# One core, three networks in a row: the overflow branch one expert earlier, weight splits in halves, the scaling behind the last hl, and a new order at the first expert

## The chip, the cores and the metric

One core of a Trainium2 chip runs the whole program in one launch. The metric is the device time of an execution in microseconds; the profiled execution also gives a span, from its first to its last instruction. TensorE is called PE in the rows (PEld is its weight load), VectorE DVE, ScalarE ACT, GpSimd POOL, and SP issues most DMAs.

## The reference

Three computations follow each other, all in float32: a recurrent attention (4 batches, 8 heads, 768 positions, 40 channels a head), a network of eight experts of which each token uses one, and a network shared by all 3072 tokens. Cut to what matters here:

```python
def _moe_ref(x, w_gate, w_output_gate, w1, w2):        # x: 3072 x 320
    logits = x @ w_gate
    e_idx = np.argmax(logits, axis=1)
    ...                                                 # gate_w: softmax of the best, eom: sigmoid
    for e in range(8):
        mask = e_idx == e
        h = np.maximum(x[mask] @ w1[e], 0.0)            # 320 -> 1024
        ye = h @ w2[e]                                  # 1024 -> 320
        out[mask] = gate_w[mask, None] * eom[mask, e, None] * ye

def _moe2_ref(x, w_in, w_out, alpha):
    h = x @ w_in                                        # 320 -> 2048
    g = np.maximum(h, 0.0) + alpha * np.minimum(h, 0.0)
    return g @ w_out                                    # 2048 -> 320
```

## The kernel before, in words

Float32 products are made of fast ones: each operand is split into a rounded part (hi, hh, xh) and the rest (lo, hl, xl), and three products of the parts are summed. ScalarE makes the rounded part by a copy, VectorE the rest by a subtraction. So every weight matrix is loaded raw by a DMA (`raw`, three buffers), then split by a *job* (`piece.split`: one ScalarE copy, L309, and one subtraction, L310). A job that is done issues the next load. Jobs of the next expert run during the present one. `conv` jobs turn the shared network's 64-bit weights into float32 on the way and write them back to memory from GpSimd's queue (L330 to L332).

Tokens are first routed. Each group of tokens goes through the steps `best` (one-hot of the best expert, small VectorE operations), `count` (two matmuls with the one-hot, L156), `place` (row numbers, L166 to L175), `scatter` (an indirect DMA from GpSimd to the rows of the buffer `xs`, L177), then `sums` and `scale` (the factor `sc`). Only the last groups are routed behind the attention, in `go`, between the first expert's steps (`route`).

The experts are *blocks* of 8 steps f, of 448 tokens each; expert 0 has 384 tokens as the first block and 128 as the ninth. The shared network then runs as six blocks c of 512 tokens and 16 steps. In `run` a step is: first-layer matmuls into one of three hp buffers (`mm1`, L394), the activation with its split into hh and hl (L399 and L402 for experts, L408 to L411 for the shared network), the second-layer matmuls (`mm2`, L421) of the step two before, and then the hooks of this f: jobs, loads, transposes of the next block's x (`xparts`: L383, L384, L386), and so on. Engines work strictly in the order in which this is written down, and SP's and GpSimd's DMAs start in that order too.

Behind expert 7 all steps are drained, and `overflow` stands there: a count is read into a register of every engine, and if it is over zero, tokens beyond an expert's room are worked off; with these inputs the branch is not entered. Then `gather2` fetches the first 512 tokens of the shared network from `xs` by four indirect DMAs (L508), which must wait for expert 7's last store (L472), while the short ninth block runs. `sc0` scales them by `sc` (L514, and a copy of 64 columns, L515), the ninth block is drained at once (`flush`), and their transposes follow. In later blocks the same is done with the next 512 tokens: gather at f=0, scaling at f=4, transposes at f=6, 9 and 12 into a buffer of their own (`tp`).

## Time and profile before

| | us |
|---|---|
| three runs | 975.82, 979.36, 985.04 |
| median | 979.36 |
| the profiled execution, its own time | 975.97 |
| its span | 974.20 |
| TensorE busy in the span | 923.4 (95%) |
| VectorE, ScalarE, GpSimd busy | 758.5, 401.5, 157.0 |
| mean granted clock of TensorE | 0.978 of 2.4 GHz |

Until about 376 us the attention runs, which the change leaves alone; the first expert's block until 405, the others until 595, the short ninth block until 613, then the shared network. Busy matmul time is modelled at its end, so a stretch that looks full of matmuls can still hold time that they wait; the distance from one step's first matmul to the next tells more.

### The profile page before, as it was taken

Reading aid. Unit: us, or ns where it says so; the run is one execution under the profiler, and the core shown is the slowest. Engines: PE = TensorE matmul, PEld = TensorE weight load, DVE = VectorE, ACT = ScalarE, POOL = GpSimd, SP = SyncE. Lnnn points to the kernel's source line nnn. Section 1 sums busy time; section 2 is a strip of 40 time slices with the busy share of each in tenths; the row PEclk is TensorE's granted clock in tenths of the full one; section 3 lists DMA queues with packets and bytes.
Section 4 is the critical chain, followed back from the end, with each engine's and each line's share of the span. In section 5 each row is a group of like instructions: output and inputs, shape, how many; then the busy total and the mean of one; then the engine's idle time right before and its main releaser. Section 6 shows DMA issues by size and latency. Waiting matters only on the chain. (4 is left out here: it accounts for less than half of the span.)

```text
span 974.2 us, 26737 instructions
## 1 busy us (share of the span) xinstructions
PE 923.4 (95%) x11176; PEld 840.7 (86%) x11176; DVE 758.5 (78%) x1715; ACT 401.5 (41%) x823; POOL 157.0 (16%) x246
## 2 busy tenths in 40 slices
PE   6479999999999999999999999999999999999998
PEld 5368888888888889899999998879999999999997
DVE  7999999999998556788888885776766666666664
ACT  3745545555553454565556554332121221222211
POOL 1000000111022114144434453101010010100000
PEclk7689999999999999999999999999999999999999
DMA  4435886444434652767677776310010010000000
GB/s 126 122 105 160 247 254 189 128 123 141 136 78 102 197 149 96 256 208 249 221 236 242 236 231 207 101 45 28 28 28 28 1 54 1 28 28 1 28 1 27
DMA packets 59582, 118.45 MB, mean 122 GB/s; under 512 B 7684, under 2 KB 34500, under 8 KB 59460
## 3 DMA queue, kind: packets, MB, share of 16 engines
q1 hardware_dynamic: 55412, 103.04, 35.0%
q0 software_dynamic: 4048, 13.69, 4.2%
q8 instruction: 88, 1.44, 0.6%
q14 instruction: 34, 0.28, 0.1%
HBM read 90.24 MB, written 26.46 MB: 120 GB/s over the span
## 5 line engine op out<-in xcount | busy, mean ns | idle before, releaser
L394 PE MATMUL hp<-xh,w 128*128 128x512 f32 (+3 forms) x1008 | 298.1, 378 | 0.1
L421 PE MATMUL yp<-w,hh 128*128 128x320 f32 (+1 forms) x1280 | 284.4, 309 | 0.7 <-ACT hh L410 0.7
L421 PEld LDWEIGHTS yp<-w,hh 128*128 128x128 f32 (+1 forms) x1280 | 216.9, 185 | 11.6 <-ACT hh L410 2.3
L394 PEld LDWEIGHTS hp<-xh,w 128*128 128x128 f32 x1008 | 187.6, 189 | 26.6 <-issue 0.4
L421 PE MATMUL yp<-w,hl 128*128 128x320 f32 x584 | 181.4, 311 | 3.9 <-DVE hl L402 2.7
L410 ACT CAST hh<-g 128x512 fp32r<-128x512 f32 x96 | 59.5, 620 | 275.4 <-PE yp L421 148.4
L394 PE MATMUL hp<-xl,w 128*128 128x512 f32 (+3 forms) x336 | 127.0, 378 | 0.2 <-DVE xl L386 0.2
L411 DVE TENSOR_TENSOR hl<-g,hh 128x512 fp32r<-128x512 f32 x96 | 66.5, 693 | 72.8 <-ACT hh L410 72.0
L421 PEld LDWEIGHTS yp<-w,hl 128*128 128x128 f32 x584 | 109.6, 188 | 6.3 <-DVE hl L402 3.4
L408 DVE TENSOR_SCALAR g<-hp,al 128x512 f32<-128x512 f32 x96 | 71.8, 748 | 39.8 <-PE hp L394 39.8
L310 DVE TENSOR_TENSOR w<-raw,w 128x1024 fp32r<-128x1024 f32 (+3 forms) x65 | 87.5, 1347 | 17.8 <-ACT w L309 15.5
L409 DVE SCALAR_TENSOR_TENSOR g<-hp,g 128x512 f32<-128x512 f32 x96 | 66.4, 691 | 3.3
L394 PEld LDWEIGHTS hp<-xl,w 128*128 128x128 f32 x336 | 63.4, 189 | 5.7 <-DVE xl L386 0.6
L309 ACT CAST w<-raw 128x1024 fp32r<-128x1024 f32 (+1 forms) x66 | 64.3, 976 | 8.2 <-DMA raw<-W 8.1
L692 DVE TENSOR_TENSOR tmp<-S 128x30 f32<-128x30 f32 (+27 forms) x258 | 63.6, 271 | 1.0
L694 DVE TENSOR_TENSOR S<-S,tmp 128x30 f32<-128x30 f32 (+27 forms) x258 | 63.6, 271 | 0.9
L508 POOL DMA_INDIRECT xg<-xs,pos x24 | 25.9, 1078 | 226.5 <-PE tp L383 167.8
L819 PE MATMUL Pp<-rz,xt 128*128 128x128 f32 x384 | 55.3, 287 | 0.0
L789 ACT COPY x<-W 32x320 f32<-32x320 f32 x96 | 40.0, 417 | 30.4 <-PE W L786 26.9
L399 ACT ACTIVATE hh<-hp 128x448 fp32r<-128x448 f32 (+2 forms) x72 | 36.7, 509 | 36.4 <-issue 22.8
L819 PEld LDWEIGHTS Pp<-rz,xt 128*128 128x128 f32 x384 | 46.4, 191 | 2.5 <-issue 0.2
L820 DVE TENSOR_TENSOR x<-Pp,mask 128x512 f32<-128x512 f32 x48 | 32.4, 686 | 18.0 <-PE Pp L819 15.9
(169 smaller groups left out, 1362.9 us busy)
## 6 DMA issues: line engine op xcount, KB each, us to landing
raw<-W SPq DMA_DIRECT2D x45, 512.0 KB
x<-VX SPq DMA_DIRECT2D x48, 232.0 KB
xs<-z SPq DMA_DIRECT2D x17, 480.0 KB
fm<-FM SPq DMA_DIRECT2D x46, 160.0 KB
raw<-WI SPq DMA_DIRECT2D x10, 512.0 KB
raw<-WO SPq DMA_DIRECT2D x10, 512.0 KB
vv<-VM SPq DMA_DIRECT2D x24, 160.0 KB
rz<-R SPq DMA_DIRECT2D x48, 80.0 KB
```

Source lines behind the costliest of these rows:

```text
L309: s.nc.scalar.copy(hi,r[0][:,0:n])
L310: (eng or s.nc.vector).tensor_tensor(lo,r[0][:,0:n],hi.bitcast(F32),SUB)
L394: for i,(l,r) in enumerate(seq): nc.tensor.matmul(hp,l,r,start=(i==0),stop=(i==len(seq)-1))
L408: nc.vector.tensor_scalar(g,hp,0.0,s.al[:,f:f+1],ALU.min,MUL)
L409: nc.vector.scalar_tensor_tensor(g,hp,0.0,g,ALU.max,ADD)
L410: nc.scalar.copy(hh,g)
L411: nc.vector.tensor_tensor(hl,g,hh.bitcast(F32),SUB)
L421: nc.tensor.matmul(yp[j][o],l,r[:,f],start=(f==0 and i==0),stop=(f==nf-1 and i==len(p)-1))
L692: V.tensor_tensor(t3[0][:,r],S[:,r,j:j+1].to_broadcast([P,n,w]),S[:,j:j+1,j+1:].to_broadcast([P,n,w]),MUL)
L694: for r in parts(split): V.tensor_tensor(S[:,r,j+1:],S[:,r,j+1:],t3[0][:,r],ADD)
L789: k=nc.scalar.copy(x[bl,sd,:,64:192].rearrange("p a (j d) -> p a j d",j=2)[:,:,:,0:40],W[bl].rearrange("p (a j) d -> p a j d",j=2))
L819: nc.tensor.matmul(Pp[:,2*qq:2*qq+2],xt[:,qq,128*sd:128*sd+128],rz1[:,:,qq,sd],start=True,stop=True)
```

## The change

It has six parts, all in the part behind the attention.

1. `overflow` is called behind expert 6 instead of expert 7, so that the blocks are run as 0 to 6, branch, 7, and then the rest.
2. In the last step of a block with a tail of 64 tokens `mm2` does the tail first, and `done` copies and stores it first.
3. Expert 7's eight jobs go to f = 0, 0, 1, 2, 2, 3, 4, 5 instead of one to each f. The three jobs of the ninth block are split in halves of 512 columns, one at each f from 0 to 5, and two of its three loads go to the beginning of the shared network.
4. The scaling of the first 512 tokens stands behind the activation of the ninth block's last step (`soon`), half on VectorE and half on ScalarE. In the shared network all scaling is on ScalarE, at f = 9 to 12 of its first block, behind the weight splits, and at f = 5 to 8 of the later ones.
5. The transposes of the next 512 tokens stand together at f=13, two of the three parts in hp buffers.
6. At the first expert the transposes of its x stand ahead of `best`, and `count` and `place` move into the block's second step. The first piece of its second weight is split in two parts on VectorE, not on GpSimd and ahead of the block. The load of expert 1's rows goes from GpSimd's queue to SP's; the transposes of these rows stand together at f=6.

```diff
-            i=(nc.gpsimd if e==1 else nc.sync).dma_start(out=xg[0:m,js,0:D],in_=src)
+            i=nc.sync.dma_start(out=xg[0:m,js,0:D],in_=src)
...
-        def split():
-            hi,lo=dst()
-            s.nc.scalar.copy(hi,r[0][:,0:n])
-            (eng or s.nc.vector).tensor_tensor(lo,r[0][:,0:n],hi.bitcast(F32),SUB)
+        def split(a=0,b=n):
+            hi,lo=dst(); c=slice(a,b)
+            s.nc.scalar.copy(hi[:,c],r[0][:,c])
+            s.nc.vector.tensor_tensor(lo[:,c],r[0][:,c],hi[:,c].bitcast(F32),SUB)
...
+    def part(s,a,b,end=True):
+        s.jobs[s.ndone][1](a,b); s.ndone+=end
...
-        for j in range(J):
+        for j in range(J) if f<nf-1 or n%128==0 else (J-1,*range(J-1)):
...
                 late.append((b,f,b["act"](hp,f)))
+                for fn in b.get("soon",{}).get(f,[]): fn()
                 while len(late)>(0 if f==b["nf"]-1 and b.get("flush") else 2): fin()
...
         s.push(s.mix(s.wexpert(1),s.convs(0)))
-        s.job()
...
+        for fn in X[0][2]: fn("hp")
         while rq[0][1].__name__!="count": route()
-        for fn in X[0][2]: fn("hp")
-        route()
         s.pre()
...
-                for dst,m,js in r:
+                for dst,m,js in r[::-1]:
...
             if e==0:
-                hooks[0].append(lambda: route())
-                hooks[1].append(lambda: route(1000))
-                hooks[1].append(lambda: load(1)); hooks[4].append(lambda: next(cnt))
+                hooks[0].append(lambda: s.part(0,D,False))
+                hooks[1]+=[lambda: route(4),lambda: s.part(D,1024),s.load]
+                hooks[2].append(lambda: load(1)); hooks[3].append(lambda: route(1000)); hooks[4].append(lambda: next(cnt))
...
-            n=6+len(s.convs(e)) if e<NE else 3
-            for i in range(n+2 if e==0 else n): hooks[(1,2,3,4,5,6,7,7)[i] if e==0 else (i*8+7)//n if e<NE else i].append(s.job if e<NE else lambda: s.job(False))
+            n=6+len(s.convs(e)) if e<NE else 0
+            if e==NE:
+                for i in range(6): hooks[i].append(lambda i=i: s.part(512*(i%2),512*(i%2)+512,i%2))
+                hooks[1].append(s.load)
+            for i in range(n+2 if e==0 else n): hooks[(2,2,3,4,5,6,7,7)[i] if e==0 else (0,0,1,2,2,3,4,5)[i] if e==NE-1 else (i*8+7)//n].append(s.job)
             if e==0:
-                for k in (2,1,0): hooks[(6,7,7)[k]].insert(0,lambda k=k: X[1][2][k](('tp','tp','hp')[k]))
+                for k in (2,1,0): hooks[6].insert(0,lambda k=k: X[1][2][k](('tp','hp','hp')[k]))
...
-        s.run(blocks[:NE])
+        s.run(blocks[:NE-1])
         s.overflow()
+        s.run(blocks[NE-1:NE])
...
-                nc.vector.tensor_scalar(xg[:,j,0:D],xg[:,j,0:D],s.sc[:,n:n+1],None,MUL)
-                nc.vector.tensor_copy(xg[:,j,D:384],xg[:,j,256:D])
+                if c or j%2:
+                    nc.scalar.activation(xg[:,j,0:D],xg[:,j,0:D],AF.Copy,scale=s.sc[:,n:n+1])
+                    nc.scalar.copy(xg[:,j,D:384],xg[:,j,256:D])
+                else:
+                    nc.vector.tensor_scalar(xg[:,j,0:D],xg[:,j,0:D],s.sc[:,n:n+1],None,MUL)
+                    nc.vector.tensor_copy(xg[:,j,D:384],xg[:,j,256:D])
...
-        for f in (3,4,5): blocks[NE]["hooks"][f].append(s.load)
-        for j in range(4): blocks[NE]["hooks"][min(j+5,7)].append(lambda j=j: sc0(j))
+        blocks[NE]["soon"]={7:[lambda j=j: sc0(j) for j in range(4)]}
...
-                if c==0: s.job()
+                if c==0: s.load(); s.load(); s.job()
...
-                hooks[4]+=[lambda sc=sc,j=j: sc[0](j) for j in range(4)]
-                for k in range(3): hooks[6+3*k].append(lambda k=k,c=c: X[NE+2+c][2][k]())
+                for j in range(4): hooks[j+(5 if c else 9)].append(lambda sc=sc,j=j: sc[0](j))
+                hooks[13]+=[lambda k=k,c=c: X[NE+2+c][2][k](tags[k]) for k in range(3)]
```

On SP's queue behind the attention (`raw` are weights, `xg` the rows of expert 1), before:

```order
L212 DMA xa<-xs 128x3x320
L306 DMA raw<-W 128x1024 x5
L306 DMA raw<-W 128x512
L306 DMA raw<-W 128x1024 x2
L317 DMA raw_7482<-WI 128x1024
```

and now:

```order
L212 DMA xa<-xs 128x3x320
L306 DMA raw<-W 128x1024
L212 DMA xg<-xs 128x3x320
L212 DMA xg<-xs 64x320
L306 DMA raw<-W 128x1024 x4
```

The load of expert 1's rows, which GpSimd issued, now stands behind one weight load and ahead of all others.

On VectorE at the end of the ninth block (`hl` of its last steps, `xg` the gathered rows), before:

```order
L402 SCALAR_TENSOR_TENSOR hl<-hp,hh 128x128 x3
L514 TENSOR_SCALAR xg<-xg,sc 128x320
L515 COPY xg<-xg 128x64
L402 SCALAR_TENSOR_TENSOR hl<-hp,hh 128x128
L514 TENSOR_SCALAR xg<-xg,sc 128x320
L515 COPY xg<-xg 128x64
L402 SCALAR_TENSOR_TENSOR hl<-hp,hh 128x128
L514 TENSOR_SCALAR xg<-xg,sc 128x320
```

and now:

```order
L310 TENSOR_TENSOR w_9803<-raw,w_9802 128x512
L404 SCALAR_TENSOR_TENSOR hl<-hp,hh 128x128 x2
L523 TENSOR_SCALAR xg<-xg,sc 128x320
L524 COPY xg<-xg 128x64
L523 TENSOR_SCALAR xg<-xg,sc 128x320
L524 COPY xg<-xg 128x64
L388 TENSOR_TENSOR xl<-tp,xh 128x512 x2
```

No hl stands behind a scaling any more, and only two of the four scalings are left there.

On SP from expert 7's stores to the shared network's weights (`wi`, `wo`), before:

```order
L306 DMA raw<-wi_65 64x1024 x2
L472 DMA xs<-yo 128x320 x3
L472 DMA xs<-yo 64x320
L235 TENSOR_LOAD nbi
L306 DMA raw<-wo_66 128x3x320 x2
L306 DMA raw<-wi_65 128x1024
L473 DMA xs<-yo 128x320
```

and now:

```order
L306 DMA raw<-wi_65 64x1024 x2
L473 DMA xs<-yo 64x320
L473 DMA xs<-yo 128x320 x3
L306 DMA raw<-wo_66 128x3x320
L474 DMA xs<-yo 128x320
L306 DMA raw<-wo_66 128x3x320
L306 DMA raw<-wi_65 128x1024 x2
```

The read of the count (L235) is gone from here, and two of three weight loads went behind the ninth block's own store (L473 before, L474 now).

## Rows read from the trace of the kernel before

**Rows 1.** Stages: window, length, PE, PEld, DVE, ACT, POOL busy (count), clock, DMA share, GB/s.

```profile
376.00:405.00 29.00, 26.43 (x162) 24.44 (x161) 20.52 (x50) 15.55 (x31) 10.04 (x18) 1.00 0.49 161
405.00:595.00 190.00, 190.00 (x1141) 181.53 (x1139) 157.12 (x274) 108.16 (x180) 81.18 (x78) 1.00 0.72 232
595.00:613.00 18.00, 14.54 (x102) 13.37 (x102) 8.84 (x22) 7.08 (x17) 4.87 (x4) 0.93 0.60 197
613.00:655.00 42.00, 40.03 (x201) 32.65 (x201) 32.77 (x49) 14.31 (x20) 3.83 (x4) 0.99 0.27 80
```

**Rows 2.** Timeline, first expert: start, duration, engine, line, operation [idle before <-releaser].

```profile
377.86 0.39 PE L156 MATMUL pr<-ohs,one 128*128 128x16 f32 x2 [0.83 <-DVE ohs L153]
379.94 2.40 POOL L310 TENSOR_TENSOR w<-raw,w 128x1024 fp32r<-128x1024 f32 x1 [1.52 <-ACT w L309]
381.04 1.33 DVE L166 TENSOR_TENSOR add<-tot,base 128x8 f32<-128x8 f32 x1
...
385.43 0.96 POOL L177 DMA_INDIRECT xs<-xu,pos  x1 [0.21 <-issue]
...
388.50 1.38 POOL L212 DMA_DIRECT2D xg<-xs  x2 [2.03 <-PE hp L394]
...
396.29 0.83 PE L383 MATMUL tp<-ident,xg 128*128 128x128 f32 x4 [1.10 <-DMA xg<-xs]
```

**Rows 3.** Two-microsecond windows at the end of the ninth block, columns as in rows 1.

```profile
608.00:610.00 2.00, 0.06 (x1) 0.06 (x1) 0.90 (x4) 0.00 (x0) 0.00 (x0) 1.00 0.37 142
610.00:612.00 2.00, 1.92 (x10) 1.68 (x11) 0.98 (x5) 1.01 (x2) 0.00 (x0) 0.65 0.15 54
612.00:614.00 2.00, 2.00 (x8) 1.73 (x7) 1.67 (x3) 1.61 (x3) 0.79 (x1) 0.50 0.08 28
```

**Rows 4.** Timeline, from expert 7's end to the shared network's first transposes.

```profile
594.68 0.46 PE L421 MATMUL yp<-w,hh 128*64 128x320 f32 x2
594.88 0.43 ACT L470 COPY yo<-yp 128x320 f32<-128x320 f32 x1 [0.45 <-PE yp L421]
...
600.69 1.98 POOL L508 DMA_INDIRECT xg<-xs,pos  x1 [7.62 <-DMA xs<-yo]
...
605.52 0.96 POOL L508 DMA_INDIRECT xg<-xs,pos  x1 [0.30 <-issue]
...
609.07 0.39 DVE L514 TENSOR_SCALAR xg<-xg,sc 128x320 f32<-128x320 f32 x1 [1.93 <-DMA xg<-xs,pos]
...
609.60 0.28 DVE L402 SCALAR_TENSOR_TENSOR hl<-hp,hh 128x128 fp32r<-128x128 f32 x1
...
609.94 0.41 PE L421 MATMUL yp<-w,hl 128*128 128x320 f32 x1 [2.02 <-DVE hl L402]
610.19 2.75 PE L383 MATMUL tp<-ident,xg 128*128 128x128 f32 x12
```

**Rows 5.** The chain that ended last, at expert 7's last store: start, length, what.

```profile
596.29 3.46 DMA xs<-yo
```

**Rows 6.** The line L508: the gathers' time from issue to landing.

```profile
DMA to landing us min/median/max: 2.9/3.1/4.4
```

**Rows 7.** Timeline, shared network: VectorE's and TensorE's steps, later transposes.

```profile
612.59 0.77 PE L394 MATMUL hp<-xh,w 128*128 128x512 f32 x1
...
618.52 0.74 DVE L408 TENSOR_SCALAR g<-hp,al 128x512 f32<-128x512 f32 x1
...
620.56 0.39 PE L394 MATMUL hp<-xh,w 128*128 128x512 f32 x1
...
622.71 0.74 DVE L408 TENSOR_SCALAR g<-hp,al 128x512 f32<-128x512 f32 x1
...
624.15 0.39 PE L394 MATMUL hp<-xh,w 128*128 128x512 f32 x1
...
657.34 0.45 PE L421 MATMUL yp<-w,hh 128*128 128x320 f32 x2
662.69 0.60 PE L383 MATMUL tp<-ident,xg 128*128 128x128 f32 x4
```

## What I predict

> **What bounds the kernel now.** I read the stages first [rows 1]. TensorE is busy in every stage behind the attention, and where it isn't, it waits for something that this change touches: 2.57 of 29.00 us idle around the first expert, none in 190 us over the experts after it, 3.46 of 18.00 us at the passage to the last network. The first block of the last network shows 1.97 us idle, but there busy time hides more (below). So all that can be gained behind the attention lies in three places, and 190 us of dense matmuls can only lose.
>
> First place [rows 2]: at 377.86 TensorE has waited 0.83 us for the one-hot, because the routing's small VectorE steps stand ahead of the split of x. At 396.29 it has waited 1.10 us for the second expert's rows. Their load went out on GpSimd's queue at 388.50, when the last scatter (385.43) had landed, and took until 396.3 beside weight loads. GpSimd's split of weights ran from 379.94 for 2.40 us, and VectorE's first step of the placement, which moves 128x8, took 1.33 us beside it.
>
> Second place [rows 4, 5]: the last expert's matmuls end at 594.68+0.46 = 595.14; its last store is issued at 596.29 and lands 3.46 us later; the gathers start at 600.69 and the fourth at 605.52; one landing ends only at 609.07. In VectorE's order the last hl of the short block stands behind that scaling (609.60), so TensorE waits 2.02 us until 609.94 and transposes from 610.19. Then its clock is down: 0.65 and 0.50 in the two stretches of 2 us after the one with 0.06 us busy [rows 3]. That is the 1.2 GHz level for some 4 us. The wait of 1.10 us at 396.29 brought no such drop: the clock of its whole stage is 1.00 [rows 1].
>
> Third place [rows 7]: a step of the last network is 3.59 us on TensorE (620.56 to 624.15), but 4.19 us on VectorE when it also splits weights (618.52 to 622.71; the rest of the nine such steps repeat it, 4.2 to 4.3). The lead of two steps is used up after three. From the second-layer matmuls of f=1 (1.83 us after 620.56, so 622.39) to those of f=9 (657.34) TensorE needs 34.95 us; eight steps of 3.59 and two groups of transposes at 0.44 would be 29.6. So 5.3 us go there, though the matmul view shows them mostly as stretched matmuls.
>
> **The change part by part.**
>
> First expert. The transposes' split now stands ahead of the best-of search, and counting goes behind the second step. TensorE gets 0.83 us earlier to the first matmul, but the split itself (three VectorE steps of 0.5 us) still ends about 0.4 us after; and the two counting matmuls (0.47 us) move, they don't vanish. I take 0.4 us. The weights' split leaves GpSimd; VectorE pays about 1.2 us for it in two parts (0.4 before, 0.8 behind the placement) and gets back the 1.17 us of the slowed step. Nothing of that is on TensorE's path: its second-layer matmuls start some 2 us later. The second expert's load moves to SP's queue: there it waits for the scatters and **holds every weight load behind it**, all of the second expert's but the first. Scatter to landing took 3.1 us (385.43 to 388.50); the scatters come about 0.4 us earlier. The load then goes ahead of two weight loads (0.56 and 1.0 MB), at some 340 GB/s about 391 instead of 396.3, so the 1.10 us go. Late are now the weights: the second piece at about 392.5, the third at about 394. ScalarE is in order, so the seventh hh waits behind the third piece's cast, and the grouped transposes use two of the three hp buffers, so the eighth step's first matmul waits for that hl: my sum has it at 397.2 instead of 395.8. Of the 2.57 us idle and some 0.9 us of stretched matmuls I count **2.0 us** as gained; bounds 0.5 (scatters land 1.2 us later) and 3.2 (weights come in time).
>
> Overflow branch. It moves from behind expert 7 to behind expert 6. That drains TensorE once at each end, where it was pipelined before; the drained steps need hl of the last step 3.2 us after its matmul, and VectorE has two short splits in between, so I price the drain at 0. Work is what it was. Expert 7's eight splits move into its first six steps; counting 1.2 us per split, 2.4 per conversion and 0.8 per hl, VectorE ends each hl 1.2 to 2 us ahead of need. Queued behind the branch on SP are four of expert 7's loads, behind expert 6's store; they need their buffer anyway, about 2 us after SP is through. I take **-0.3 us** for one contended step; bounds 0 and -3.
>
> Passage. The tail of 64 rows is now copied and stored first, so the last store waits for one ScalarE copy (0.43 us, like the one at 594.88 [rows 4]): 595.65 instead of 596.29. Only one weight load is in flight beside it instead of three, and two of the next three stand behind the short block's own store. Landing: between 2.9 (the best gather) [rows 6] and the 3.46 seen; I take 3.0, so 598.65. First gather 0.94 us later, as seen (599.75 to 600.69): 599.6. The fourth follows 4.83 us later as seen, or 3.8 without the first one's double time (1.98 us): 603.4 to 604.4. Landing 3.1, the median [rows 6], gives 606.5 to 607.5. Scaling of the last quarter on ScalarE with its copy: 0.43+0.2 and a handover, 0.8, so 607.3 to 608.3. TensorE without its stalls would be at the transposes at 610.19-3.2 = 607.0; hl no longer waits for a gather. Three transposes fit in, then 0.3 to 1.3 us are left to wait, too short by the row above for the clock to fall. The twelve transposes took 2.40 us at the lower clock (610.19 to 612.59, the next matmul), about 1.05 us at the upper. The last network's first matmul comes at 608.1 to 609.0: **4.0 us** gained, bounds 1 and 4.8.
>
> The ScalarE step itself is not in the trace of before. The Trainium skill ("ScalarE: Activation LUTs", Rules for kernel authors) says to use VectorE, not ScalarE, for a multiply, and in What ACT_TABLE_LOAD costs gives 186 ns plus 0.833 ns an element, with 93 ns for a pointer operand: as an estimate from that page 0.55 us for 320 columns and 0.24 for 64, so 0.79 instead of my 0.63, and the sum would be 0.2 us less. No run here shows it yet.
>
> First block of the last network. Scaling leaves VectorE (four times 0.39+0.20 [rows 4] = 2.4 us), and the split of the next x moves behind the weights, to f=13. VectorE's chain decides until f=9: its first step came 5.5 us after the transposes' start (618.52-2.82-610.19); at the upper clock I take 4.55. Then 2.87 us each for f=0 and 1, 4.19 (four times), 4.31 (three times), 3.5 with the last, short split: hl of f=9 at 43.5 us, its matmuls 0.3 before. Counted from the network's first matmul, 1.05 us in, that is 42.1 us; before it was 657.34-612.59 = 44.75. Then twelve transposes and a wait for the hp buffer, 1.35, against the one group left before, 0.44: **1.7 us** gained. It is not the whole 5.3: 3.5 us of it are the eight weight splits, which stay. ScalarE's four scalings (0.63 each by my price above) stand at f=9 to 12, behind the steps with a weight split, and fit beside the activation's copy, so it is no new bound. Bounds 0.5 and 4.
>
> Later blocks. Transposes in one group instead of three save two switches, about 0.2 us in each of four (0.60 us busy for a group of four [rows 7]); scaling was hidden before and is now: **0.8 us**, bounds -1 and 1.
>
> **Sum.** 2.0-0.3+4.0+1.7+0.8 = 8.2 us. The profiled execution took 975.97 us (span 974.20 and 1.77 around it), so 967.8. That is at the fast end of the three runs shown (975.82 to 985.04); their median is 3.4 above it. I put half of that on top: **969 us**.
>
> **The rivals.**
> A. *The gather still ends last.* All its parts stay as seen: 595.65+3.46+0.94+4.83+4.4 (the worst landing [rows 6]) is 609.3, scaling 610.1: no earlier than now, one idle stretch of 3 us and the lower clock again. What is left is 2.0-0.3+1.7+0.8, 4.2: 971.8 by the profile, 973.5 with the shift. For it: three loads were seen beside the slow landings, one is still there. Chance 0.18.
> B. *The weights come late.* Four loads behind the scatters in expert 0, or behind SP's branch in expert 7, cost what rows 2 gave: 0.5 and -3 there and 4.0 in all: 972.0, or 973.7. Chance 0.12.
> C. *More of the third place goes*, since with the scaling gone the lead of two steps lasts longer: 3.5 us more, 964.3, or 966. Chance 0.1.
> D. *Slower: the hp ring stops the last network.* The grouped transposes take two of the three hp buffers in five blocks. The matmuls of f=14 need the buffer of f=13; TensorE is there 2.8 us after f=13 (1.75+1.05), VectorE frees it 1.44 us (0.75+0.69) after it starts on it. The slack is 1.4 us. It costs whatever VectorE lags beyond that, in each block; the whole gain is used up at 8.2/5 = 1.6 us, so it decides from a lag of 3.0. In the first block I have a lag of 1.6 there; later ones split no weights and VectorE needs 2.9 of 3.59 us. At a lag of 5 it would be 975.97-8.2+18 = 986. Chance 0.06.
> That the change moves nothing (the stores' order and the branch being without effect) is in A.
>
> **How the numbers follow.** The forecast has 0.54. A measurement of this kernel tells about 1%, 9.8 us, from no change; the shown runs differ by as much. My 8.2 by the profile or 10 by the median lies on that border: of the forecast and C about 0.4 are faster by over 1%; A, B and the rest of the forecast are within; D and a bad spread give slower 0.05. The range runs from 2 us under C on the profile's base (962; the bounds of the first two places allow them) to A and B with the whole gap to the median on top (977).
>
> **What would show it.** Right: the second expert's load lands before 392 and TensorE's wait at the first expert's transposes is under 0.5 us; expert 7 stays dense; the gathers start before 600 in terms of before; the transposes run at clock 1.00, with hl ahead of the scaling; the step of the first shared block is still 4.2 us on VectorE but no transposes wait for scaling. Wrong: a wait over 1.5 us at the transposes (A), ScalarE waiting for raw weights in experts 0 or 7 (B), TensorE waiting at f=14 in each block (D).

## The result, and the profile after

The changed kernel takes 982.42 us in the median of 20 runs (978.02 to 991.03), the kernel before 977.23 (973.81 to 985.04). The ratio is 1.0056, with a 95% interval of 1.0039 to 1.0074: **slower by half a per cent**, where 1% faster was forecast.

Both profiles are cut at the same five groups of matmuls, each taken by its start in the timeline: (A) from the first expert's own transposes to the first transposes that stand in the second expert's block; (B) the six periods of 8 steps from there to the first transposes in expert 7; (C) from there to the ninth block's first matmul; (D) the passage, to the last network's first matmul; (E) to the end of the span.

| us | ahead of A | A | B | C | D | E | span |
|---|---|---|---|---|---|---|---|
| before | 375.88 | 38.40 | 164.19 | 16.82 | 17.30 | 361.61 | 974.20 |
| after | 376.44 | 42.96 | 167.99 | 20.98 | 14.91 | 359.62 | 982.90 |
| difference | +0.56 | +4.56 | +3.80 | +4.16 | -2.39 | -1.99 | +8.70 |
| forecast | 0 | -2.0 | 0 | +0.3 | -4.0 | -2.5 | -8.2 |

Over the 20 profiles of this study the stretch ahead of A, which no kernel here changes, ran from 370.95 to 381.59, so a single execution carries up to 10 us that the change has no part in. Each part is therefore read below from its own stage.

**A.** The timeline of the changed kernel in the first expert; here [rows 2] had a wait of 0.83 us and one of 1.10.

```profile
378.10 0.44 PE L396 MATMUL hp<-xh,w 128*128 128x384 f32 x1 [0.51 <-DVE xl L388]
...
383.82 0.16 DVE L175 TENSOR_TENSOR pos<-pl,m 128x2 int32<-128x2 f32 x1
...
384.75 0.96 POOL L177 DMA_INDIRECT xs<-xu,pos  x1 [5.71 <-ACT w L309]
...
386.01 1.21 POOL L177 DMA_INDIRECT xs<-xu,pos  x1 [0.21 <-issue]
...
389.90 1.23 SPq L212 DMA_DIRECT2D xg<-xs  x2
391.22 1.49 SPq L306 DMA_DIRECT2D raw<-W  x3
...
397.53 1.04 ACT L309 CAST w<-raw 128x1024 fp32r<-128x1024 f32 x1 [7.13 <-DMA raw<-W]
...
399.75 0.55 DVE L404 SCALAR_TENSOR_TENSOR hl<-hp,hh 128x384 fp32r<-128x384 f32 x1
...
400.45 1.09 PE L385 MATMUL tp<-ident,xg 128*128 128x128 f32 x4 [4.35 <-DVE hl L404]
```

Three weight loads leave together at 391.22, behind the rows' load. ScalarE gets the first only at 397.53. Its next hh, and with it VectorE's hl, come behind that cast, and that hl must free the hp buffer of the last of the twelve transposes. TensorE waits 4.35 us, and then, by windows (columns as in rows 1), its clock is at the 1.2 GHz level for some six microseconds:

```profile
400.00:402.00 2.00, 1.13 (x5) 0.76 (x5) 2.00 (x4) 1.69 (x6) 0.34 (x1) 0.55 0.58 133
402.00:404.00 2.00, 2.00 (x6) 2.00 (x7) 1.94 (x4) 1.05 (x2) 0.07 (x1) 0.50 0.74 229
404.00:406.00 2.00, 2.00 (x8) 2.00 (x8) 1.44 (x2) 1.08 (x2) 0.00 (x0) 0.50 0.23 55
406.00:408.00 2.00, 2.00 (x10) 1.95 (x10) 1.63 (x2) 0.96 (x2) 0.00 (x0) 0.74 0.80 246
```

**B.** The timeline at two block ends; the kernel before had no row with a wait here.

```profile
469.44 0.47 DVE L469 TENSOR_TENSOR yo<-yp,yo 64x320 f32<-64x320 f32 x1
469.63 0.46 PE L423 MATMUL yp<-w,hh 128*128 128x320 f32 x2
469.84 0.47 DVE L470 COPY yo<-yp 128x320 f32<-128x320 f32 x1
470.36 0.56 PE L423 MATMUL yp<-w,hh 128*128 128x320 f32 x2
...
495.67 2.35 DVE L310 TENSOR_TENSOR w<-raw,w 128x1024 fp32r<-128x1024 f32 x1 [0.93 <-ACT w L309]
...
498.93 0.47 DVE L470 COPY yo<-yp 128x320 f32<-128x320 f32 x1
...
499.46 0.56 PE L423 MATMUL yp<-w,hh 128*128 128x320 f32 x2 [1.50 <-DVE yo L470]
```

The tail's addition (L469) stands ahead of the copy (L470) that frees the second quarter of yp. The next block's second pair of second-layer matmuls would start 0.43 us after the first; it starts 0.73 after it, as soon as the copy is done. Where VectorE is late for another reason, the wait is 1.50.

**C.** The timeline in expert 7; the kernel before was dense here.

```profile
585.65 0.43 DVE L325 TENSOR_SCALAR qt<-raw 128x512 uint32<-128x512 uint32 x1 [1.67 <-DMA wo<-lf]
...
588.58 4.21 DVE L310 TENSOR_TENSOR w<-raw,w 128x1024 fp32r<-128x1024 f32 x2
589.58 2.13 POOL L331 TENSOR_TENSOR lf<-lf,qt 128x512 f32<-128x512 f32 x1
...
592.72 0.54 DVE L404 SCALAR_TENSOR_TENSOR hl<-hp,hh 128x384 fp32r<-128x384 f32 x1
...
593.32 0.27 DVE L388 TENSOR_TENSOR xl<-tp,xh 128x128 fp32r<-128x128 f32 x1
...
593.65 0.33 PE L385 MATMUL tp<-ident,xg 128*128 128x128 f32 x1 [2.76 <-DVE xl L388]
```

The bunched jobs put a conversion and two splits between two hl on VectorE; the two splits take 4.21 us beside GpSimd's part of the conversion. Here too the clock falls (0.69 and 0.50 from 594 to 598).

**D.** The timeline of the passage; ahead of the transposes [rows 4] had one wait of 2.02 us.

```profile
608.22 2.08 SPq L473 DMA_DIRECT2D xs<-yo  x4
...
614.28 1.03 POOL L513 DMA_INDIRECT xg<-xs,pos  x1 [13.83 <-PE hp L396]
...
618.16 0.96 POOL L513 DMA_INDIRECT xg<-xs,pos  x1 [0.30 <-issue]
618.58 0.56 ACT L520 ACTIVATE xg<-xg,sc 128x320 f32<-128x320 f32 x1 [0.48 <-DMA xg<-xs,pos]
619.18 0.24 ACT L521 COPY xg<-xg 128x64 f32<-128x64 f32 x1
...
620.27 0.33 PE L385 MATMUL tp<-ident,xg 128*128 128x128 f32 x1 [0.74 <-DVE xg L523]
...
621.74 1.90 PE L385 MATMUL tp<-ident,xg 128*128 128x128 f32 x9 [1.14 <-ACT xg L520]
```

The last hl is out of the way, but TensorE still waits for the third and the fourth quarter of x.

**E.** The last network, for [rows 7]: second-layer matmuls of f=9 and the grouped transposes.

```profile
665.25 0.45 PE L423 MATMUL yp<-w,hh 128*128 128x320 f32 x2
...
674.19 1.47 PE L385 MATMUL tp<-ident,xg 128*128 128x128 f32 x12
675.42 0.48 PE L396 MATMUL hp<-xh,w 128*128 128x512 f32 x1
```

From the first matmul (623.28) to f=9 it is 41.97 us instead of 44.75; a whole block is 58.82 instead of 58.83.

### The profile page after: what moved, and what is told of

Read it like the earlier page. It is cut to its first block, busy times and chain, and to the rows that moved or that the text cites. A ratio compares the mean times of both kernels' runs of the same rounds, so it can differ in the third digit from the quotient of the medians.

```text
span 982.9 us, 26744 instructions
## 1 busy us (share of the span) xinstructions
PE 927.7 (94%) x11176; PEld 845.8 (86%) x11176; DVE 749.7 (76%) x1676; ACT 417.8 (43%) x871; POOL 149.4 (15%) x243
## 5 line engine op out<-in xcount | busy, mean ns | idle before, releaser
L309 ACT CAST w<-raw 128x1024 fp32r<-128x1024 f32 (+3 forms) x70 | 64.9, 930 | 8.8 <-DMA raw<-W 8.7
L513 POOL DMA_INDIRECT xg<-xs,pos x24 | 23.8, 990 | 233.5 <-ACT xh L386 162.2
```

The source lines that it names most:

```text
L309: s.nc.scalar.copy(hi[:,c],r[0][:,c])
```

## Experiments: one part undone at a time

**e1**, the tail last again in all blocks but expert 7:

```diff
-for j in range(J) if f<nf-1 or n%128==0 else (J-1,*range(J-1)):
+for j in (J-1,*range(J-1)) if tail and f==nf-1 and n%128 else range(J):   # tail: e==NE-1
-for dst,m,js in r[::-1]:
+for dst,m,js in r[::-1 if e==NE-1 else 1]:
```

> The changed kernel, but only the last expert's 64-row tail is worked and copied first; in all other blocks it is last again. Theory (the tail's two VectorE steps now stand ahead of the copy that frees the second quarter of yp, and the next block's first second-layer matmuls wait for it): the wait of 0.30 us behind the first quarter at each of the seven block ends goes, and the 1.50 us at 499.46 shrinks by some 0.4 us to about 1; the period from block to block is 27.37 us again instead of 27.73; in all 2.0 to 3.4 us less than the changed kernel, about 979.5. Rival (the 3.4 us that experts 1 to 6 lost came from VectorE's splits, which are slower beside GpSimd): the period stays at 27.7, the time at 982.

B is 164.67, with five periods of 27.37 to 27.47 (before 27.34 to 27.39); only the last, into expert 7, keeps 27.72, as in every later run with the branch behind expert 6 (27.70 to 27.80): there the pipeline is drained for the branch, and C is 0.3 us shorter for it (e3). The theory holds: B is 3.3 us shorter than in the changed kernel's profile, and 1.7 to 2.1 shorter than in the eight other profiles that have the tail first and the branch in that place. The time, 981.7 us (1.005 of before, 1.003 to 1.007), does not tell 2 us from the spread.

**e2**, the rows' load on GpSimd's queue, at its new place:

```diff
-i=nc.sync.dma_start(out=xg[0:m,js,0:D],in_=src)
+i=(nc.gpsimd if e==1 else nc.sync).dma_start(out=xg[0:m,js,0:D],in_=src)
```

> The changed kernel, but the load of the second expert's rows is issued from GpSimd's queue again, at its new place. Theory (on SP's queue it held three weight loads until 391.22 us, they landed together at 397.5, ScalarE in order waited 7.13 us for the first): the weight loads go out at about 385 to 388 us, ScalarE waits under 2 us there, TensorE's wait of 4.35 us at the grouped transposes falls under 1.5 us, and the half clock until 407 goes: 4 to 6 us less than the changed kernel, about 977.5. Rival (the grouped transposes, two of three in hp buffers, make the wait): a wait of 3 us or more stays, and the time is within 1 us of 982.

Neither. A falls to 40.65. The weights come in time, and the rows don't. First GpSimd's timeline, then TensorE's:

```profile
390.39 1.37 POOL L212 DMA_DIRECT2D xg<-xs  x2 [4.91 <-DMA xs<-xu,pos]
...
397.22 1.01 PE L385 MATMUL tp<-ident,xg 128*128 128x128 f32 x4 [3.83 <-DMA xg<-xs]
```

The last scatter went out at 384.18, and its rows are free only 6.2 us later, beside weight loads that nothing holds now. Time 981.21 (1.0034, 1.0015 to 1.0053).

**e3**, expert 7's jobs even, and **e4**, the branch behind expert 7 again:

```diff
-(0,0,1,2,2,3,4,5)[i] if e==NE-1 else (i*8+7)//n
+(i*8+7)//n                                        # e3
-s.run(blocks[:NE-1]); s.overflow(); s.run(blocks[NE-1:NE])
+s.run(blocks[:NE]); s.overflow()                  # e4
```

> The changed kernel, but expert 7's eight weight jobs stand one at each step again, with the branch still behind expert 6. Theory (the bunched jobs: two splits and a conversion in a row on VectorE, the splits at 2.1 us beside GpSimd instead of 1.2, behind a load that came late): the wait of 2.76 us at 593.65 and the half clock behind it go, 4 to 5 us less than the changed kernel, about 978. Rival (the branch drains the engines and holds SP's loads): a wait of 2 us or more stays in expert 7, time within 1.5 us of 982.

> The changed kernel, but the overflow branch stands behind expert 7 again. Rival of the runs before (the branch holds expert 7's loads): the wait of 2.76 us in expert 7 is gone or under 1 us, and the passage to the last network is longer than 14.75 us (608.53 to 623.28, from the last expert's last matmul to the last network's first) by under 1 us: 3 to 5 us less than the changed kernel, about 978.5. Theory (it is the bunched jobs): the wait in expert 7 stays above 1.5 us and the passage grows by 0 to 2 us: 982 to 984.

e3: no wait in expert 7, C is 16.47, and the time is 976.8 us, that of before (1.0001, 0.9981 to 1.0021). e4: C itself is 16.81, but TensorE now waits at the block end ahead of it, 1.80 and 0.59 us: the last period of B is 31.81 us instead of 27.7, and the time stays at 982.21 (1.0049, 1.0031 to 1.0068). The passage is 14.84, as with the branch ahead. So the jobs are the cause, whichever side the branch stands on, and the branch itself costs and brings nothing (in e3, 0.35 us more in B and 0.35 less in C).

**e9**, the bunched jobs without GpSimd's share (`pool` is false for the two conversions in expert 7):

```diff
-nc.gpsimd.tensor_tensor(lf,lf,q,MUL)
-nc.gpsimd.tensor_tensor(lf,lf,Af,ADD)
+if pool: nc.gpsimd.tensor_tensor(lf,lf,q,MUL); nc.gpsimd.tensor_tensor(lf,lf,Af,ADD)
```

> The changed kernel, but GpSimd's two operations (multiply, add) in the two conversions that run during expert 7 are left out, so a part of the last network's second weight matrix is not converted and the output there is not the reference's; loads, VectorE's and ScalarE's work and the stores stay. Asked: of the wait of 2.76 to 3.47 us in expert 7, what comes from VectorE's two splits beside GpSimd (2.0 us each instead of 1.2) and what from the conversion's load, which came 1.45 us after VectorE was free? If the slow splits are most of it: splits of 1.2 us, the wait at 1.5 us or less, and from the seventh expert's last transposes to the ninth block's first matmul under 19 us, instead of 21 to 23.2. If it is the late load: the wait stays at 2.2 us or more, and the stretch at 20 us or more.

The two splits take 1.2 us each, the wait is 1.30 and C is 18.01, although the conversion's load is as late as before (ScalarE waits 3.61 us for it, in the changed kernel 3.14). From VectorE's and TensorE's timelines:

```profile
590.53 2.35 DVE L310 TENSOR_TENSOR w<-raw,w 128x1024 fp32r<-128x1024 f32 x2
...
593.73 0.33 PE L386 MATMUL tp<-ident,xg 128*128 128x128 f32 x1 [1.30 <-DVE xl L389]
```

By this one profile most of the loss is VectorE beside GpSimd; the 1.5 us over e3's 16.47 that are left are the bunching itself.

**e5**, the whole first block as before (part 6 undone), **e6**, e5 with the edits of e1 and e3, and **e7**, e6 with the first x ahead of `best`:

```diff
+for fn in X[0][2]: fn("hp")                       # e7
 while rq[0][1].__name__!="count": route()
-for fn in X[0][2]: fn("hp")
 route()
```

> The changed kernel, but the first expert's block as in the kernel before (part 6 undone whole: order, splits, queue, transposes). Theory (part 6 as a whole costs what the first expert lost): from the first expert's first matmul to the second expert's first transposes 36 us again, instead of 41.3 in the changed kernel's profile and 39.0 to 40.7 in the four runs so far; the 0.8 us won ahead of it are given back: 3 to 4.5 us less than the changed kernel, about 978.5. Rival (loads of weights are late there whatever the order, since the profiles differ by which load lands last): 38 us or more, time 980.5 or above.

> The changed kernel with three things undone: the first expert's block as before, the tail first only in the last expert, expert 7's jobs one at each step. The branch, the passage and the last network stay as changed. If the stages add up (first expert 36, six experts 27.37 each, expert 7 to its end 16.5, passage 14.8, last network 359.6 us): 4.9 us less than the kernel before, about 972, ratio 0.995. Rival (what one stage wins the next gives back): within 1.5 us of the kernel before.

> The run before it, but with the one step of part 6 that won something: the transposes of the first expert's x stand ahead of the best-of search, while counting and placing stay where they were before. If the 0.8 us ahead of the first matmul come from that alone and the scatters are not later: 0.8 us less than the run before it, about 971.2. Rival (the scatters come later by the split's three VectorE steps, and the rows of the second expert with them): the first expert takes 0.5 to 1.5 us more, and the time is the same or above.

e5: A is 38.79, time 978.21 (1.0035, 1.0009 to 1.0062): part 6 as a whole is the loss in A. e6: 971.19 us against 974.92 on the same chip, ratio **0.9957 (0.9929 to 0.9984)**, the stages as expected but for the passage (15.47 for 14.8). e7: 973.64 (0.9975, 0.9951 to 0.9999), A 40.40: its counting matmuls still stand ahead of the first expert's, and TensorE waits 2.60 us for their one-hot. The rival holds: the second scatter leaves 11.31 us into A, in e6 9.54, and the rows' load lands as much later.

**e8**, the changed kernel with x of the later blocks scaled at f=4 and transposed at f=6, 9 and 12, the scaling still on ScalarE; and **e11**, e6 with VectorE scaling it, at f=4:

```diff
-hooks[j+(5 if c else 9)].append(lambda sc=sc,j=j: sc[0](j))
+hooks[4].append(lambda sc=sc,j=j: sc[0](j))                             # e8, e11
-hooks[13]+=[lambda k=k,c=c: X[NE+2+c][2][k](tags[k]) for k in range(3)]
+for k in range(3): hooks[6+3*k].append(lambda k=k,c=c: X[NE+2+c][2][k]())  # e8
-if c or j%2:
+if c==0 and j%2:                                                        # e11
```

> The changed kernel, but in the last network the next x is scaled at the fourth step and transposed in three groups at the sixth, ninth and twelfth into the buffer of their own, as before; the scaling stays on ScalarE. Theory (in the first block of the last network VectorE's chain sets the pace until the ninth step; two of the three splits of x, 0.69 us each, come back into it): from the last network's first matmul to the end 0.8 to 1.6 us more than the 359.6 of the changed kernel, time about 983.5. Rival (the 2.0 us came from the scaling alone): 359.6 again; the other way (grouping itself costs, since two of three hp buffers are taken): 359 or less.

> The combined kernel, but in the last network VectorE scales the next x, at the fourth step, as before; the transposes stay together at the thirteenth. Theory (in the first block VectorE's chain sets the pace until the ninth step, and the scaling, four times 0.6 us, is a part of it): from the last network's first matmul to the end 1.5 to 2.4 us more than the 359.75 of the combined kernel. Rival (the place of the transposes or of the weights' loads made the 2.0 us): 360.3 or less.

e8: E is 359.37 (time 981.4, 1.0056, 1.0026 to 1.0086): neither grouping the transposes nor scaling later does anything. e11: E is 361.75, 2.0 more than e6's 359.75 and as long as before (361.61), while the 18 profiles with the scaling on ScalarE have 359.4 to 360.7. TensorE is stopped in the first block (timeline):

```profile
637.47 0.56 PE L423 MATMUL yp<-w,hh 128*128 128x320 f32 x2 [2.11 <-ACT hh L412]
```

So the whole gain of E is the scaling that left VectorE (time 975.42; 0.9993, 0.996 to 1.0027).

**e10**, e6 with the scaling ahead of the last hl, and **e12**, e6 with the tail last in expert 7 too:

```diff
-blocks[NE]["soon"]={7:[lambda j=j: sc0(j) for j in range(4)]}
+for j in range(4): blocks[NE]["hooks"][min(j+5,7)].append(lambda j=j: sc0(j))  # e10
-tail=e==NE-1
+tail=False                                                              # e12, e18
-for dst,m,js in r[::-1 if e==NE-1 else 1]:
+for dst,m,js in r:                                                      # e12, e18
```

> The combined kernel (first block as before, tail first in the last expert alone, expert 7's jobs even), but the first scaling stands where it stood before: behind the steps f=5, 6 and 7 of the ninth block, ahead of the last hl on VectorE and of the last hh on ScalarE. Theory (the order alone makes TensorE wait in one piece before the transposes, and the clock falls behind that wait): one wait of 2 us or more ahead of the last second-layer matmuls, the clock at 0.5 in the stretch after it, and from the ninth block's first matmul to the last network's first 16 to 17.5 us instead of 14.7 to 15.5. Rival (the passage got shorter because the gathers land sooner, with fewer weight loads beside them): 15.5 us or less.

> The combined kernel, but the 64-row tail comes last in expert 7 too, as before. Theory of the prediction (with the tail first the last store, and so the gathers, start some 0.6 us earlier): from the ninth block's first matmul to the last network's first 0.4 to 1 us more than in the combined kernel (15.5). Rival (SP issues the four stores one after the other, 0.53 us each, so the order of the copies does not matter, or the tail first delays the other three): the same within 0.3 us, or less.

e10 (973.96; 0.997, 0.9944 to 0.9995): D is 16.12, in three waits of 0.89, 0.81 and 0.39 us and not one, with the clock at 0.54 and 0.60 from 606 to 610. That is neither the theory's one wait nor the rival's 15.5, and e5 and e7, with the new order, have 16.13 and 16.11. The length goes by when the fourth gather lands and by what the clock does: in the eight profiles in which it stays at 1.00 until the last network's first matmul, this matmul comes 1.74 to 1.80 us after that landing, in the eleven others of the new passage 2.18 to 2.48, e10 among them with 2.45. The order of scaling and hl shows no effect of its own there; all 19 are shorter than 17.30.

e12 (973.04; 0.9972, 0.9948 to 0.9997): D is 14.74, no longer than with the tail first. With the branch behind expert 6 the last of the four stores leaves 1.46 to 1.53 us into the stage when the tail is first, and at 1.31 or 1.32 when it is last (e12, e18 below): SP issues them one after the other. When the first gather starts does not follow from that: at 5.49 in e12, 6.42 in e18, 5.91 in the changed kernel and 6.61 in e6.

**e13 to e17**, what in the first block costs. e13 and e14 are e2 with one half of the order undone each, e14's half being the weight splits (the first on GpSimd ahead of the block, the others one step earlier); e15 is e6 with the rows on SP's queue, the reverse of e2's edit; e16 is the changed kernel with the transposes apart, and e17 is e15 with the reverse of that.

```diff
-hooks[0].append(lambda: s.part(0,D,False))
-hooks[1]+=[lambda: route(4),lambda: s.part(D,1024),s.load]
-hooks[2].append(lambda: load(1)); hooks[3].append(lambda: route(1000))
+hooks[0]+=[lambda: s.part(0,D,False),lambda: route()]                   # e13
+hooks[1]+=[lambda: route(1000),lambda: load(1),lambda: s.part(D,1024),s.load]
-hooks[6].insert(0,lambda k=k: X[1][2][k](('tp','hp','hp')[k]))
+hooks[(6,7,7)[k]].insert(0,lambda k=k: X[1][2][k](('tp','tp','hp')[k]))  # e16
```

> The changed kernel with the rows' load on GpSimd's queue and the routing one step earlier (counting behind the first step, placing, scatters and the rows' load behind the second, ahead of the weight split); the split of the first weights on VectorE and the grouped transposes stay. If the late routing makes the other half: from the first expert's transposes to the second expert's first ones 38.4 to 39.3 us, instead of 40.65 with the queue alone undone. If the weight splits do: 40 us or more.

> The changed kernel with the rows' load on GpSimd's queue and the weight splits as before (the first on GpSimd ahead of the block, the others one step earlier); the routing stays late and the transposes grouped. If the weight splits make the other half (they set when raw buffers come free, and so when weight loads go out beside the scatters): 38.4 to 39.3 us from the first expert's transposes to the second expert's first ones. If the late routing does: 40 us or more, and the scatters land as late as in the run with the queue alone undone.

> The combined kernel (whole first block as before), but the rows' load on SP's queue. If the queue costs by itself (it holds the weight loads until the scatters have landed): ScalarE waits for raw weights in the first expert, and from its transposes to the second expert's first ones it takes 1.5 to 3 us more than the 39.06 of the combined kernel. If the queue only costs together with the late routing: within 0.7 us of 39.06; the prediction's sum for the queue (rows at 391 instead of 396, weights a little later) would give 37 to 38.5.

> The changed kernel, but the transposes of the second expert's rows stand apart again: one group behind the seventh step, two behind the eighth, in the buffers of before. If the grouping turns ScalarE's wait into TensorE's (the last group's hp buffer needs the hl that waits for the weights, and the eighth step's matmuls, which could fill the wait, stand behind it): TensorE's longest wait under 2 us, the clock stays up, and from the first expert's transposes to the second expert's first ones 38 to 40 us instead of 41.3 to 43.2. If not: a wait of 3 us or more and 41 us or more.

> The kernel of e15 (combined kernel, rows' load on SP's queue) with the transposes of the second expert's rows grouped behind the seventh step, as the change has them. If the grouping is what costs: a TensorE wait of 2 us or more there, and from the first expert's transposes to the second expert's first ones 40 us or more instead of 38.13. If it is not: 38 to 39 us, as before.

| | changed | e2 | e13 | e14 | e16 | e5 | e6 | e15 | e17 |
|---|---|---|---|---|---|---|---|---|---|
| A, us | 42.96 | 40.65 | 39.77 | 42.02 | 39.52 | 38.79 | 39.06 | 38.13 | 37.73 |
| first block | new | new | routing early | old splits | transposes apart | before | before | before | before |
| rows on | SP | GpSimd | GpSimd | GpSimd | SP | GpSimd | GpSimd | SP | SP |

(Times: e13 981.16, 1.0045, 0.9996 to 1.0094; e14 985.36, two runs; e15 975.0, 0.9975, 0.9936 to 1.0014; e16 979.67, 1.0043, 1.0015 to 1.0071; e17 974.52, 0.9975, 0.9952 to 0.9997.) The first block of before with the rows on GpSimd's queue is in six profiles, whose A is 38.33 to 39.88, so a difference of 1 us between single profiles tells little. In the old order SP's queue and the grouping cost nothing; e17 even has the lowest A. In the new order, whose A was 41.32 to 43.15 in six profiles, either costs: ungrouped (e16), the last step's matmuls fill the wait, and TensorE's longest stops are these (timeline):

```profile
398.30 0.56 PE L423 MATMUL yp<-w,hh 128*128 128x320 f32 x2 [0.95 <-ACT hh L401]
...
399.63 0.41 PE L423 MATMUL yp<-w,hl 128*128 128x320 f32 x1 [0.78 <-DVE hl L404]
```

The clock falls behind them as well, to 0.59 and 0.56 from 400 to 404, which was not expected.

So it is a product of three: weights that come some 2 us later than in e15 (ScalarE has them 21.1 us into A, there 19.15), TensorE 0.5 us earlier at the transposes (18.62 us into A, there 19.14), and nothing left to do beside the grouped transposes. e13 and e14 don't split the rest into one cause. In e13 the scatters leave later, not earlier (the second 10.56 us into A, in e2 9.57), but no weight load goes until 11.59, and the rows' load can follow the scatter after 3.1 us instead of 6.2. In e14 the second scatter leaves at 10.84 and it is 6.1 us again, with two weight loads sent from 9.70 on. The rows' load goes at 13.66, 15.78 and 16.93 us in e13, e2 and e14, and A follows in that order.

**e18**: e15 with the tail last everywhere.

> The version that the runs point to: first block as before but the rows' load on SP's queue, tail last everywhere, expert 7's jobs even; of the change there stay the branch behind expert 6, the scaling behind the last hl and on ScalarE, the later weight loads, the half splits and the grouped transposes of the last network. By its stages (38.2 and 37.1 us to the second and from it on as in the combined kernel): 971 to 972.5 where the kernel before has 977, ratio 0.994 to 0.997.

973.3 us against 975.51, ratio 0.9958 (0.9937 to 0.9979), C 16.51, D 16.08. e6 and e18 both beat the two kernels, by 0.4% of the kernel before, and the runs don't tell them apart.

## Why the prediction was wrong, step by step

Of the 8.2 us that were forecast the passage brought 2.4 and the last network 2.0. Three terms turned round: the first expert (2.0 gained in the sum, 4.6 lost), the tail first (no cost in the blocks, 3.5 lost), and expert 7's jobs (0.3 lost in the sum, 4.2 measured).

- **The tail first** was priced only at the last store. It stands in a function that all blocks share, and there it puts the tail's addition ahead of the copy that frees yp: 0.3 us at each block end and more where VectorE is late. B lost 3.80 us (2.1 to 2.5 in eight other profiles), 0.35 of it by the branch. No rival had it. Its gain was no gain either (e12): "595.65 instead of 596.29" left out that SP's stores queue in order behind the tail's.
- **Expert 7's jobs**: "counting 1.2 us per split ... VectorE ends each hl 1.2 to 2 us ahead of need" took the split's duration without GpSimd beside it. It was 2.1 there, and C lost 4.16 us (2.6 to 6.4 in the other profiles with bunched jobs where C shows it) against a bound of 3. Rival B had the place, but for late weights behind SP's branch and not for slow splits; it took the bound of 3 there, let the first expert still gain 0.5, and so kept a gain of 4.0 in all. It left out the clock, which fell behind each wait. The Trainium skill ("SBUF — State Buffer", Who interferes with whom) says that a VectorE instruction with two SBUF inputs contends with a GpSimd instruction that reads SBUF; that is this pair, and the trace agrees: 4.21 us for two splits, 2.35 without GpSimd's work (e9). The branch itself was priced rightly, at 0.
- **First expert**: three steps failed. "The scatters come about 0.4 us earlier": their positions do, 7.54 us after the transposes' start instead of 7.98, but the first scatter leaves 0.76 us behind them instead of 0.28, and the second 9.57 us in, before 9.55. That step is 0.76 in all nine profiles in which VectorE splits the first piece, and 0.28 in the eleven in which GpSimd does; what holds the scatter there, the rows don't show. "The second piece at about 392.5, the third at about 394" took loads one after the other; three left within 1.1 us, and the first was usable 6.3 us after its issue, at 397.53. And the hp ring, seen as 397.2 instead of 395.8, gave 401.95 (401.4 as counted before): a wait of 4.35 us and then the lower clock. Rival B had late weights here, at a far smaller price. The queue alone, in e15, brought the rows about as summed, ready 16.2 us into A instead of 20.4; but ScalarE waits 5.74 us for weights there too, and A is 38.13, only 0.3 us below before's.
- **Passage**: the path was right, two of its sizes were not: 2.39 us for 4.0. The early start did not come: the last store leaves 1.46 us into D, before 1.00, and the first gather starts 4.45 us after it, before 4.40. What came is the fourth gather: issued 9.79 us into D, before 10.23, it takes 2.94 us instead of 4.38, about as forecast (3.1), and lands 1.88 us earlier in all. The 4.4 us of [rows 6] was not the longest landing. The chains that ended last wait for the second gather before and the fourth after (start, length, what):

```profile
602.97 6.07 DMA xg<-xs,pos
```

```profile
618.16 2.94 DMA xg<-xs,pos
```

Two weight loads moved behind; that this is the reason was not tried alone. And "too short for the clock to fall" was wrong: in this profile it fell behind the waits of 0.74 and 1.14 us, and from the landing to the last network's first matmul it took 2.19 us, before 2.69, where the sum had 1.5 to 1.6.

- **Scaling on ScalarE**: 0.56+0.24 = 0.80 us where the sum had 0.63. The Trainium skill ("ScalarE: Activation LUTs", What ACT_TABLE_LOAD costs) gave an estimate of 0.79, and the trace agrees.
- **First block of the last network**: 44.75-41.97 = 2.78 us up to f=9 for the forecast 2.65, and with the transposes behind it 1.99 for 1.7: right, and e11 with e8 shows the cause. **Later blocks**: 0.8 forecast, 0.01 us a block measured.
- Rival D did not come: at f=14 TensorE waits nowhere.

## What to carry to other kernels

Ask of every reordered line which other blocks run it; a reorder meant for the last block is paid in all of them. Where engines work in order, a row's duration is valid only beside the neighbours it was measured with, and bunching work changes the neighbours. When the whole time scatters by 1%, cut the profiles at the same instructions and compare stages: parts of 2 us, and parts that cancel, are plain there. Know the spread of a stage first, from profiles in which it is the same program: for A here it was 1.5 us.

## What the runs showed of the hardware

- VectorE's 128x1024 subtraction takes 1.2 us alone (e9) and 2.1 beside GpSimd's operations on 128x512; GpSimd's own take 1.28 to 2.16 us.
- The same kind of waits in the passage had two outcomes for TensorE's clock. Windows over the passage of the changed kernel, and then of e6, with waits of 0.92, 0.76 and 1.12 us:

```profile
620.00:622.00 2.00, 0.59 (x3) 0.40 (x4) 0.41 (x2) 0.85 (x3) 0.00 (x0) 1.00 0.16 56
622.00:624.00 2.00, 2.00 (x11) 1.98 (x10) 1.18 (x2) 1.71 (x4) 0.10 (x1) 0.52 0.42 93
624.00:626.00 2.00, 2.00 (x7) 1.56 (x6) 1.64 (x3) 1.15 (x2) 1.69 (x2) 0.63 0.89 261
```

```profile
608.00:610.00 2.00, 0.66 (x2) 0.28 (x2) 0.58 (x2) 0.30 (x2) 0.00 (x0) 1.00 0.29 90
610.00:612.00 2.00, 1.46 (x10) 1.15 (x10) 0.37 (x1) 1.97 (x6) 0.00 (x0) 1.00 0.01 4
```

Why it fell in one and not in the other, these rows don't say.
- The load that waits for a scatter's rows could go 3.1 us after the scatter's issue with the DMA engines at a share of 0.27 (before), and 6.2 us after it at a share of 0.88, with weight loads sent beside it (e2).
- GpSimd's first scatter left 0.28 us behind its positions where GpSimd itself had split weights before it (before, e14), and 0.76 behind them where that split was VectorE's and GpSimd had been idle for 5.7 us (changed kernel, e2). Why, these rows don't say.
